# The last V load of a cached-attention decode kernel, cut into parts whose rows are placed on chosen DMA engines

## The chip, the cores and the metric

The kernel runs on one core of a Trainium2 chip. The metric is the device time of one execution in microseconds (us), as the median of several runs. The kernel before takes 1277.13 us (three runs, 1277.09 to 1277.35).

## The reference

One decode step for a batch of four tokens with 512 features: a pre-normed attention over a long key/value cache, then a pre-normed gated feed-forward block, both with a residual.

```python
B, Sq, D = 4, 1, 512;  H, Sk, Dh = 32, 8192, 128;  F = 1792
q = (layernorm(x) @ wq)                                # per head, 128 wide
p = softmax(einsum("bhqd,bhkd->bhqk", q, k_cache) * Dh ** -0.5)
h = x + einsum("bhqk,bhkd->bhqd", p, v_cache) @ wo
n = layernorm(h)
out = h + (sigmoid(n @ w_gate) * (n @ w_up)) @ w_down
```

All inputs are bf16. The two caches hold 4 x 32 x 8192 x 128 elements each, 537 MB together. The weights add 4 MB (wq), 4 MB (wo) and 5.5 MB (gate, up, down).

## The kernel before

The work on the cache is cut into 32 groups g of four heads of one batch item. For each group one K of 8 MB and one V of 8 MB are loaded, each with one DMA instruction from SyncE's queue (SP): 128 partitions, one row of 32768 elements (64 KB) on each. Partition p holds 256 positions of head p // 32 of the group. SBUF holds three such slots (the tensor `KV`, three times `SLOT` = 32768 elements per partition), which K and V loads use in turn. Loads are issued in the order K(0), K(1), V(0), K(2), V(1), K(3) and so on. Each waits for the event that frees its slot: K(g+1) for the end of group g-2's output (`t_ox`, a VectorE instruction), V(g) for group g's softmax maximum (`t_a5`, VectorE), which comes after the last use of K(g).

Of a group, VectorE transposes K in eight pieces (L332), TensorE (PE) makes the scores (L342, 64 matmuls) and, one group later, the product with V (L385, 64 matmuls), and ScalarE and VectorE do the softmax between them. Groups 2 to 30 run in a hardware loop on PE and VectorE.

The end of the program is written out by hand. `load_v(31)` (L299), the last V, waits for the output of group 29 and goes into slot 0. Its DMA counts up a semaphore of its own, `vl`. Then follow, on the same queue, `load_weights`: two halves of wo (L312), w_gate and w_up (L316), which wait for the last softmax maximum, and w_down in four loads (L326: 1 MB, 0.5 MB and twice 128 KB), which wait for the PE product of group 30. PE does the product of group 30 (L385), three filler matmuls (`fill`, L434, which keep PE busy and whose results nobody reads), then `pv_last` (L399), the 64 matmuls on the last V. `pv_last` waits for the last V's semaphore and for the softmax weights. Behind it come, one after the other: `extract_last` (L420 to L426, with a matmul at L424 that needs the tile `RS`, which GpSimd makes late in the program, L504 to L510), the first half of the output projection with wo (L457), fillers, the second half, the second layernorm, w_gate (L560), three fillers, w_up (L560), the gating, the transposed hidden vector (L571) and w_down (L591). The result leaves by a DMA from ScalarE's queue (L603).

GpSimd (POOL) has little to do: it builds identities and masks at the start, makes the masked queries of each group (L282), copies each group's output (L286), and makes `RS` at the end. It issues no DMA.

`_Prog.dma` (L79 on) issues a DMA behind its waits and lets it add 16 to its semaphore; several DMAs on one semaphore add up, and a wait for the last of them waits for all.

Of the kernel before, what the change touches and what calls it, by code (L numbers as in the profile page):

```python
# [5 lines left out]
BF16 = mybir.dt.bfloat16  # L6
FP32 = mybir.dt.float32
# [4 lines left out]
class _Prog:  # L12
# [28 lines left out]
    def emit(self, eng, fn, waits=(), incs=1, key=None, take=(), keep=True):  # L41

        todo = self._waits(eng, waits)
        assert not (todo and self.looped), (eng, todo)
        key = key or eng
        tok = self.token(key, incs) if incs else None

        def run(e):
            for k, v in todo:
                e.wait_ge(self.sems[k], v)  # L50
            for k, v in take:
                e.wait_ge(self.sems[k], v).then_inc(self.sems[k], -v)  # L52
            made = fn(e)
            made = made if isinstance(made, list) else [made]
            if incs:
                assert len(made) == incs
                for m in made:
                    m.then_inc(self.sems[key], 1)

        if keep:  # L60
            self.ops[eng].append(run)
        return tok
# [26 lines left out]
def bass_sequential_preLN__mha_block_cached__glu_gated_glu__decode_kernel(  # L89
# [20 lines left out]
    SLOT = 4 * S * DH // 128  # L110
    SCALE = float(DH) ** -0.5
    EPS = 1e-5
    LW = 144
    PW = 8 * 128 + 32

    prog = _Prog()
    emit = prog.emit

    with ExitStack() as es:
        def SB(name, shape, dt, **kw):  # L120
            return es.enter_context(nc.sbuf_tensor(name, shape, dt, **kw))

        def raw(t):
            return t.tensor if hasattr(t, "tensor") else t

        KV = SB("KV", [128, 3, SLOT], BF16, align_bytes=256)
        Lq = SB("Lq", [128, 4, LW], BF16)
        PT = SB("PT", [128, 3, PW], BF16)
        E_sb = SB("E_sb", [128, 512], BF16)
# [19 lines left out]
        OTs = SB("OTs", [128, 3, 4], BF16)  # L149
        hhT = ET[:, 0:NFT * B]  # L150
        hh = E_sb[:, :]
        dummy = SB("dumm", [128, 2], FP32)

        KVROW = 3 * SLOT

        def kv(slot, off, inner, p0=0, np_=128):
            return bass.AP(raw(KV), p0 * KVROW + slot * SLOT + off, [[KVROW, np_], *inner])
# [10 lines left out]
        FY = (bank[1], FA)  # L168

        keys = ["sp", "act", "dve", "pool", "pe", "x", "out", "cs", "wq", "wo0", "wo1", "wg", "wu", "wd0", "wd1", "wd2", "wd3",  # L170
                "sl0", "sl1", "sl2", "vl", "v0", "v1", "v2", "tp", "pt", "ex", "dv", "sc", "pv", "lq"]
        for k in keys:
            prog.sems[k] = es.enter_context(nc.semaphore("s_" + k))

# [2 lines left out]
        dram_v = lambda g: A_v_cache[g % B, 4 * (g // B):4 * (g // B) + 4, :, :].rearrange(  # L177
            "h (p r) d -> (h p) (r d)", p=32)
# [95 lines left out]
        t_v, t_et, t_pv, t_ox = {}, {}, {}, {}  # L274
# [19 lines left out]
        def load_v(g):  # L294
            last = g == NG - 1
            vslot[g] = slot = 0 if last else (2 * g + 2) % 3
            w = [t_ox[g - 2]] if last else [t_a5[g]] if g else [t_qp]
            if last:
                t_v[g] = [prog.dma("sp", "vl", lambda e: e.dma_start(kv(slot, 0, [[1, SLOT]]), dram_v(g)), w)] * 4  # L299
            else:  # L300
                t_v[g] = [prog.dma("sp", f"v{slot}", lambda e: e.dma_start(kv(slot, 0, [[1, SLOT]]), dram_v(g)), w)] * 4

# [44 lines left out]
        def softmax(g, keep):  # L347
# [14 lines left out]
            for a in range(4):  # L362
                if g < NG - 1:
                    dst = bass.AP(raw(PT), 32 * a * 3 * PW + u3 * PW + 32 * a, [[3 * PW, 32], [128, 8], [16, 2], [1, 16]])
                    src = bass.AP(raw(ET), 32 * a * 512, [[512, 32], [64, 8], [32, 2], [1, 16]])
                else:
                    dst = bass.AP(raw(PT), 32 * a * 3 * PW + u3 * PW + 4 * a, [[3 * PW, 32], [64, 16], [16, 4], [1, 4]])
                    src = bass.AP(raw(ET), 32 * a * 512, [[512, 32], [32, 16], [4, 4], [1, 4]])
# [22 lines left out]
        def pv_last(g):  # L391
            u3, slot = g % 3, vslot[g]
            for j in range(4):
                def f(e, j=j):
                    ins = None
                    for rl in range(NS):
                        off, t = 64 * rl + 16 * j, rl % 4
                        rhs = kv(slot, (4 * j * 16 + rl) * 128, [[2048, 4], [1, 128]])
                        ins = e.matmul(V_b[32 * t:32 * (t + 1), :], PT[:, u3, off:off + 32], rhs,  # L399
                                       start=(j == 0 and rl < 4), stop=(j == 3 and rl >= NS - 4),  # L400
                                       tile_position=(0, 32 * t), skip_group_check=True)
                    return ins
                t_pv[g] = emit("pe", f, [t_v[g][j]], take=[("pt", 4)] if j == 0 else [])

        def extract(g, keep):
            src = bass.AP(raw(PS), 512 * 2, [[4096, 128], [128, 4], [1, 4], [4, 32]])
# [56 lines left out]
        load_k(0)  # L463
        load_k(1)
        load_v(0)
        TURNS = (NG - 2) // 3
        assert 2 + 3 * TURNS == NG
        for g in range(NG):
# [13 lines left out]
            if g > 1:  # L482
                keep_o(g - 2)
                if g + 1 < NG:
                    load_k(g + 1)
                else:
                    load_v(g)
# [3 lines left out]
            if 0 < g < NG - 1:  # L491
                load_v(g)
# [12 lines left out]
        for a in range(4):  # L505
# [5 lines left out]
                SEL[32 * a:32 * a + B, :], identf[32 * a:32 * a + B, 32 * a:32 * a + B]), [t_rs])  # L511
        fill(3, S_b[0], [t_et[NG - 1]])
        pv_last(NG - 1)
        emit("pe", gather(range(3)), [t_oc[27], t_ox[NG - 2]])
        fill(1, S_b[0])
# [83 lines left out]
        def o_half(u):  # L599
# [3 lines left out]
        key, v = prog.dma("act", "out", lambda e: e.dma_start(  # L603
            out.rearrange("b s d -> (b s) d"), kv(0, 0, [[1, D]], 0, B)), [t_o])
# [33 lines left out]
```

## Time and profile before

| what | value |
|---|---|
| median of the runs | 1277.13 us (1277.09 to 1277.35) |
| profiled execution, first to last instruction (span) | 1275.6 us |
| the median over that span (what lies around the instructions) | 1.5 us |
| read from HBM | 550.77 MB, 432 GB/s over the span |
| PE busy | 1001.2 us (78%) |
| VectorE (DVE) busy | 701.8 us (55%) |
| ScalarE (ACT) busy | 85.2 us (7%) |
| GpSimd (POOL) busy | 22.6 us (2%) |
| granted TensorE clock | 0.918 |

The page gives no time of its own for the profiled execution but its span, so a time of a run is compared here with the span and 1.5 us. In the rows of a timeline the first number is the start from the span's beginning and the second the duration, both in us. "SPq" and "ACTq" are the instructions that issue DMAs on those queues. A bracket at a row's end tells how long the engine stood idle before it and what ended that. In the view of DMA issues the last number of a row is the time from the issue to the landing of the whole load. In the view of windows, "DMA share" is the busy share of the core's 16 DMA engines in a stretch; it does not name the engines.

### The profile page before, as it was taken

How to read it: one execution, taken by the hardware profiler on the slowest of the kernel's cores; microseconds unless marked ns; L12 is line 12 of the kernel's file. 1: busy time of each engine (PE TensorE's matmuls, PEld its weight loads, DVE VectorE, ACT ScalarE, POOL GpSimd, SP SyncE). 2: the span in 40 equal slices, each digit the busy share in tenths (PEclk: the TensorE clock that was granted, in tenths of full speed). 3: DMA queues.
4: the chain of work that ended last, by engine and by line, in shares of the span. 5: the costliest groups of instructions: out<-in, count | busy, mean ns of one | idle time of the engine just before them, and what ended most of it. 6: DMA issues, size and time to landing. Idle time of an engine off the chain costs nothing. (4 is left out here: it accounts for less than half of the span.)

```text
span 1275.6 us, 10932 instructions
## 1 busy us (share of the span) xinstructions
PE 1001.2 (78%) x4450; PEld 409.7 (32%) x4450; DVE 701.8 (55%) x737; ACT 85.2 (7%) x202; POOL 22.6 (2%) x88
## 2 busy tenths in 40 slices
PE   1598777779777788777798777797777897777888
PEld 1233323333233333223333233333233332333334
DVE  0865665446655446654456654456554466544562
ACT  0000000000000000000000000000000000000010
POOL 1000000000000000000000000000000000000000
PEclk9899888899888898888998888998888998888989
DMA  9999999999999999999999999999999999999998
GB/s 420 434 425 434 427 444 432 430 438 427 442 434 430 438 427 444 432 432 436 427 444 432 432 436 434 438 432 434 434 434 438 432 436 432 436 436 430 440 430 371
DMA packets 10669, 550.95 MB, mean 432 GB/s; under 512 B 1176, under 2 KB 1440, under 8 KB 1824
## 3 DMA queue, kind: packets, MB, share of 16 engines
q1 hardware_dynamic: 10640, 550.77, 99.8%
q8 instruction: 8, 0.13, 0.0%
q14 instruction: 5, 0.04, 0.0%
q10 hardware_dynamic: 16, 0.01, 0.0%
HBM read 550.77 MB, written 0.00 MB: 432 GB/s over the span
## 5 line engine op out<-in xcount | busy, mean ns | idle before, releaser
L332 DVE STREAM_TRANSPOSE KV<-KV 128x2048 uint32<-128x2048 uint32 x256 | 568.6, 2279 | 379.1 <-DVEq L52 379.1
L342 PE MATMUL PS<-KV,Lq 128*128 128x512 bf16 x2048 | 543.6, 417 | 258.2 <-PEq L52 257.5
L385 PE MATMUL PS<-KV,PT 128*128 128x512 bf16 x1984 | 433.2, 379 | 0.0
L342 PEld LDWEIGHTS PS<-KV,Lq 128*128 128x128 bf16 x2048 | 199.8, 104 | 601.4 <-issue 442.7
L385 PEld LDWEIGHTS PS<-KV,PT 128*128 128x128 bf16 x1984 | 193.8, 98 | 234.5
L358 ACT ACTIVATE E_sb<-PS,TS 128x512 bf16<-128x512 f32 x32 | 22.0, 688 | 1124.6 <-DVE TS L357 1124.6
L352 DVE TENSOR_REDUCE TS<-PS 128x1 f32<-128x512 f32 x32 | 22.1, 692 | 70.4 <-DVEq L52 70.4
L369 ACT ACTIVATE PT<-ET 32x256 bf16<-32x256 bf16 x128 | 52.9, 413 | 30.8 <-DVE ET L361 28.5
L361 DVE STREAM_TRANSPOSE ET<-E_sb 128x512 bf16<-128x512 bf16 x32 | 22.8, 711 | 30.7 <-DVEq L52 30.7
L412 DVE STREAM_TRANSPOSE OX<-PS 128x512 f32<-128x512 f32 x31 | 20.9, 675 | 8.6 <-DVEq L52 8.6
L282 POOL TENSOR_TENSOR Lq<-q_all,mask 128x16 bf16<-128x16 bf16 x32 | 8.4, 263 | 575.0 <-DVE TS L357 563.4
L286 POOL COPY OT<-OTs 128x4 bf16<-128x4 bf16 x30 | 5.8, 192 | 622.3 <-DVE OTs L415 622.3
L434 PE MATMUL PS<-identf 128*128 128x512 f32 (+3 forms) x30 | 13.3, 551 | 0.0
L253 PE MATMUL PS<-xnT,KV 128*128 128x4 bf16 x128 | 3.6, 166 | 9.4 <-DMA KV<-in_A_wq_dram 9.4
L353 DVE STREAM_TRANSPOSE TS<-TS 128x32 f32<-128x32 f32 x32 | 6.8, 211 | 5.1 <-DVEq L52 0.6
L357 DVE STREAM_TRANSPOSE TS<-TS 128x32 f32<-128x32 f32 x32 | 6.8, 211 | 4.7
L374 DVE STREAM_TRANSPOSE TS<-TS 128x32 f32<-128x32 f32 x32 | 6.8, 211 | 4.7
L415 DVE TENSOR_SCALAR OTs<-Or,small 128x4 bf16<-128x4 f32 x30 | 6.9, 229 | 4.5 <-DVEq L52 1.4
L373 DVE COPY TS<-small 128x32 f32<-128x32 f32 x32 | 5.8, 182 | 6.2 <-DVEq L52 3.0
L355 DVE TENSOR_SCALAR TS<-small 128x32 f32<-128x32 f32 x32 | 5.8, 181 | 4.8 <-DVEq L52 0.2
L414 DVE TENSOR_REDUCE Or<-OX 128x4 f32<-128x16 f32 x31 | 5.6, 179 | 4.5
L354 DVE TENSOR_REDUCE small<-TS 128x1 f32<-128x16 f32 x32 | 5.4, 170 | 4.7
(87 smaller groups left out, 78.1 us busy)
## 6 DMA issues: line engine op xcount, KB each, us to landing
KV<-in_A_wq_dram SPq DMA_DIRECT2D x1, 4096.0 KB, 12.4
KV<-in_A_wo_dram SPq DMA_DIRECT2D x2, 2048.0 KB, 22.1
KV<-in_B_w_gate_dram SPq DMA_DIRECT2D x1, 1792.0 KB, 28.2
KV<-in_B_w_up_dram SPq DMA_DIRECT2D x1, 1792.0 KB, 32.0
KV<-in_B_w_down_dram SPq DMA_DIRECT2D x1, 1024.0 KB, 24.2
KV<-in_A_k_cache_dram SPq DMA_DIRECT2D x32, 32.4
KV<-in_A_v_cache_dram SPq DMA_DIRECT2D x32, 34.3
KV<-in_B_w_down_dram SPq DMA_DIRECT2D x1, 512.0 KB, 25.0
```

Source lines behind the costliest of these rows:

```text
L282: emit("pool", lambda e: e.tensor_tensor(dst, src, msk, ALU.mult), [t_q, t_mk, t_lq0, t_a5.get(g - 1), t_oc.get(g - 3)], key="lq")
L332: emit("dve", lambda e: e.transpose(v, v), key="tp", take=take, keep=keep)
L342: ins = e.matmul(S_b[0], Lq[:, hp, 15 - s:15 - s + 128], rhs, start=(s == 0 and hp == 0), stop=(s == NS - 1 and hp == 3))
L352: dv(lambda e: e.tensor_reduce(TS[:, 0, 0:1], S_b[0], AX.X, ALU.max), [t_ts0] if g == 0 else [], [("sc", 1)])
L353: dv(lambda e: e.transpose(TS[:, 1, :], TS[:, 0, :]))
L358: emit("act", lambda e: e.activation(E_sb[:, :], S_b[0], ACT.Exp, bias=TS[:, 3, 0:1], scale=SCALE, accum_out=TS[:, 4, 0:1]), [t_a5[g]], ke ...
L361: t_et[g] = dv(lambda e: e.transpose(ET[:, :], E_sb[:, :]), take=[("ex", 1)], key="dve")
L369: emit("act", lambda e, dst=dst, src=src: e.activation(dst, src, ACT.Copy), [t_et[g], t_pt0 if g < NG - 1 else t_ptl], key="pt")
L385: ins = e.matmul(O_b, PT[:, u3, off:off + 128], rhs, start=(j == 0 and rl == 0), stop=(j == 3 and rl == NS - 1))
L412: emit("dve", lambda e: e.transpose(OX[:, :, :].rearrange("p (r i) x -> p r i x", r=4), src), w, key="dv", take=take, keep=keep)
L415: t_ox[g] = emit("dve", lambda e: e.tensor_scalar(dst, Or[:, :], small[:, 2 + g % 3:3 + g % 3], None, op0=ALU.mult), take=[("dv", 1)], kee ...
L434: ins = e.matmul(bk[:, 0:cols], identf[:, :], bass.AP(raw(identf), 0, [[128, 128], [0, cols // 128], [1, 128]]), start=True, stop=True, sk ...
```

## The change

Only the last V (group 31) is loaded in another way. Its rows are cut at 26624 elements: the first 52 KB of all 128 rows stay one load, and the last 12 KB (`REL` = 6144 elements) of each row go in seven sets of loads.

- From SP, ahead of the large load: rows 7, 15, 23 and 31 in one load, rows 39 and 47 in one, rows 55 and 63 in one.
- From SP, the large load of 128 rows of 52 KB, and behind it the 12 KB ends of the 64 even rows, of the 32 rows 1, 5, 9, ... and of the 16 rows 3, 11, 19, ....
- From GpSimd's queue, twice the sequence: a load of 8 x 4 bytes of x into spare columns of the tile `dummy` (`skip`), the ends of three rows, a load of 4 x 4 bytes of x, the end of one row. The rows are 71, 79, 87 and 95 the first time and 103, 111, 119 and 127 the second. These eight loads count up a new semaphore, `vp`.

So the 16 rows p = 7, 15, 23, ..., 127 have their last 12 KB in small loads. The change's description names DMA engines 0, 1, 8, 9, 10 and 15 as those that they go to. `pv_last` now waits for both semaphores, `vl` and `vp`. The wait of the loads for their slot is the same for SP and GpSimd (the output of group 29). `dummy` grows from two to six columns.

```diff
+    REL = 6 * 1024
...
-        dummy = SB("dumm", [128, 2], FP32)
+        dummy = SB("dumm", [128, 6], FP32)
...
             if last:
-                t_v[g] = [prog.dma("sp", "vl", lambda e: e.dma_start(kv(slot, 0, [[1, SLOT]]), dram_v(g)), w)] * 4
+                src = dram_v(g)
+
+                def part(eng, key, p0, st, n, lo, hi):
+                    dst = bass.AP(raw(KV), p0 * KVROW + slot * SLOT + lo, [[st * KVROW, n], [1, hi - lo]])
+                    return prog.dma(eng, key, lambda e: e.dma_start(
+                        dst, src[p0:p0 + st * (n - 1) + 1:st, lo:hi]), w)
+
+                def skip(n, c):
+                    xs = A_x.rearrange("b s (x d) -> (b s x) d", d=128)
+                    prog.dma("pool", "vp", lambda e: e.dma_start(
+                        dummy[0:n, 2 + c:3 + c].bitcast(BF16), xs[0:n, 0:2]), w)
+                for i in range(2):
+                    skip(8, 2 * i)
+                    part("pool", "vp", 71 + 32 * i, 8, 3, SLOT - REL, SLOT)
+                    skip(4, 2 * i + 1)
+                    t_vp = part("pool", "vp", 95 + 32 * i, 8, 1, SLOT - REL, SLOT)
+                for p0, n in ((7, 4), (39, 2), (55, 2)):
+                    part("sp", "vl", p0, 8, n, SLOT - REL, SLOT)
+                part("sp", "vl", 0, 1, 128, 0, SLOT - REL)
+                for p0, st in ((0, 2), (1, 4), (3, 8)):
+                    t_vl = part("sp", "vl", p0, st, 128 // st, SLOT - REL, SLOT)
+                t_v[g] = [t_vl, t_vp]
...
-                t_pv[g] = emit("pe", f, [t_v[g][j]], take=[("pt", 4)] if j == 0 else [])
+                t_pv[g] = emit("pe", f, t_v[g], take=[("pt", 4)] if j == 0 else [])
```

On SP's queue, at the end of the program, this stood before (the last V is the row with L299):

```order
L299 DMA KV<-in_A_v_cache_dram 128x32768 [waits s_dve]
L312 DMA KV<-in_A_wo_dram 128x8192 [waits s_dve]
L312 DMA KV<-in_A_wo_dram 128x8192
L316 DMA KV<-in_B_w_gate_dram 128x7168
L316 DMA KV<-in_B_w_up_dram 128x7168
```

and this stands there now (partitions x elements; L304 is `part`):

```order
L304 DMA KV<-in_A_v_cache_dram 4x6144 [waits s_dve]
L304 DMA KV<-in_A_v_cache_dram 2x6144 x2
L304 DMA KV<-in_A_v_cache_dram 128x26624
L304 DMA KV<-in_A_v_cache_dram 64x6144
L304 DMA KV<-in_A_v_cache_dram 32x6144
L304 DMA KV<-in_A_v_cache_dram 16x6144
L334 DMA KV<-in_A_wo_dram 128x8192 [waits s_dve]
L334 DMA KV<-in_A_wo_dram 128x8192
```

One issue has become seven, in front of the weights; the weights and their waits are as before.

On GpSimd, between the copy of group 29's output (L286 before, L287 now) and the memset that begins `RS` (L504 before, L526 now), this stood before:

```order
L471 MEMSET PT 128x1056
L286 COPY OT<-OTs 128x4 [waits s_dve]
L504 MEMSET KV 128x644 [waits s_pe]
L507 COPY KV<-identf 32x128 [waits s_pool]
L510 COPY KV<-identf 4x4 [waits s_pool]
```

and this stands there now:

```order
L287 COPY OT<-OTs 128x4 [waits s_dve]
L309 DMA dumm<-in_A_x_dram 8x2
L304 DMA KV<-in_A_v_cache_dram 3x6144
L309 DMA dumm<-in_A_x_dram 4x2
L304 DMA KV<-in_A_v_cache_dram 1x16x384
L309 DMA dumm<-in_A_x_dram 8x2
L304 DMA KV<-in_A_v_cache_dram 3x6144
L309 DMA dumm<-in_A_x_dram 4x2
L304 DMA KV<-in_A_v_cache_dram 1x16x384
L526 MEMSET KV 128x644 [waits s_pe]
```

Eight DMA issues have come in between; a load of a single row is written by the build as 16 pieces of 384 elements. On PE nothing moves; the first matmul of `pv_last` waits for one semaphore more (`s_vp`).

More of the change, by code (lines that the diff above doesn't have):

```diff
@@ L170, in bass_sequential_preLN__mha_block_cached__glu_gated_glu__decode_kernel @@
         keys = ["sp", "act", "dve", "pool", "pe", "x", "out", "cs", "wq", "wo0", "wo1", "wg", "wu", "wd0", "wd1", "wd2", "wd3",
-                "sl0", "sl1", "sl2", "vl", "v0", "v1", "v2", "tp", "pt", "ex", "dv", "sc", "pv", "lq"]
+                "sl0", "sl1", "sl2", "vl", "vp", "v0", "v1", "v2", "tp", "pt", "ex", "dv", "sc", "pv", "lq"]
         for k in keys:
```

## The prediction

> **What bounds the kernel now.** I read the page first, its DMA rows above all.
>
> ```profile
> DMA  9999999999999999999999999999999999999998
> ...
> q1 hardware_dynamic: 10640, 550.77, 99.8%
> q8 instruction: 8, 0.13, 0.0%
> ...
> HBM read 550.77 MB, written 0.00 MB: 432 GB/s over the span
> ```
>
> SP's queue (q1) keeps the 16 DMA engines busy for 99.8% of the span; PE is busy for 78%. The kernel lasts as long as its 550.77 MB take. One engine moves 432 / 16 = 27.0 GB/s. So the change, which moves no byte less, can only gain where engines stand idle. That is at the end, in the view of windows (us of the window, DMA share and GB/s last; GpSimd's busy time stands between):
>
> ```profile
> 1271.20:1271.60 0.40, 0.00 (x0) 1.00 1.03 402
> 1271.60:1272.00 0.40, 0.00 (x0) 1.00 0.67 266
> 1272.00:1272.40 0.40, 0.00 (x0) 1.00 0.61 225
> 1272.40:1272.80 0.40, 0.00 (x0) 1.00 0.57 197
> 1272.80:1273.20 0.40, 0.00 (x0) 1.00 0.34 108
> 1273.20:1273.60 0.40, 0.00 (x0) 1.00 0.00 0
> ```
>
> The last transfers end engine by engine. The share is full until 1271.6, then about 0.67, 0.61 and 0.57, that is 10.7, 9.8 and 9.1 engines of 16; none works after 1273.2. So about five engines are through by 1271.8, seven by 1272.6, and the other nine finish in the last 0.4 to 0.6 us. The idle share of the four stretches is 0.33 + 0.39 + 0.43 + 0.66 = 1.81, by 0.4 us: a mean engine waits 0.72 us for the last one. Perfect levelling would end the transfers 0.72 us earlier and not more.
>
> Next the path from the transfers to the end: the timeline of SP's issues and of PE (PEld loads weights), and in the view of DMA issues the time to landing of the last V and of w_up.
>
> ```profile
> 1218.39 0.33 SPq L299 DMA_DIRECT2D KV<-in_A_v_cache_dram  x1
> ...
> 1237.14 0.43 SPq L316 DMA_DIRECT2D KV<-in_B_w_up_dram  x1
> ...
> 1250.94 3.64 PE L399 MATMUL PS<-KV,PT 128*32 128x512 bf16 x64 [0.97 <-issue]
> ...
> 1266.35 2.84 PE L434 MATMUL PS<-identf 128*128 128x512 f32 x6
> ...
> 1269.15 0.53 PEld L560 LDWEIGHTS PS<-KV,hnT 128*4 128x4 bf16 x16 [0.78 <-DMA KV<-in_B_w_up_dram]
> ```
>
> ```profile
> KV<-in_A_v_cache_dram SPq DMA_DIRECT2D x1, 32.5
> ...
> KV<-in_B_w_up_dram SPq DMA_DIRECT2D x1, 1792.0 KB, 32.0
> ```
>
> The last V lands at 1218.39 + 32.5 = 1250.9, and PE begins on it at 1250.94 after 0.97 us of idleness: here a transfer ends last. From there to the end PE's own chain and the landings keep step. w_up lands at 1237.14 + 32.0 = 1269.1, and the fillers before it end at 1266.35 + 2.84 = 1269.19, so each hides the other. An earlier landing of the weights alone would therefore bring nothing, and an earlier V alone nothing either: both must move. They do move together, since an engine that is ahead in the last V is ahead in everything queued behind it.
>
> **The change, part by part.** *Row ends taken from the engines.* A row end is 6144 x 2 = 12,288 bytes, at 27.0 GB/s 0.455 us. Before, one load of 128 rows of 64 KB gives each engine eight rows. Now each gets the first 52 KB of its eight rows and, from the three loads of 64, 32 and 16 rows, 4 + 2 + 1 = 7 ends: one end less, -0.455 us on every engine. The 16 ends come back by the small loads. The large loads run on 16 engines with equal shares; if a small load of n rows runs on n engines, the SP loads of 4, 2 and 2 rows give two engines three ends each and two more engines one each, and GpSimd's give four engines two ends each. In sum: two engines +0.91 us, four +0.455, two 0, eight -0.455.
>
> The profile names no engine, so that the six receivers are the early ones is the change's statement and not my reading; the counts agree, though. Eight engines are relieved, and eight or nine are late; six receive, and five to seven are early. Early engines finish at about 1271.6, and a receiver of two net ends then finishes at 1272.5, still before the relieved late ones at 1273.2 - 0.455 = 1272.75. The relieved engines stay last, so the term is -0.455 us.
>
> *More loads on a ring.* A late engine works through four loads where it had one. The nearest rows are the small loads of w_down at the end.
>
> ```profile
> 1247.43 1.84 SPq L326 DMA_DIRECT2D KV<-in_B_w_down_dram  x4
> ```
>
> ```profile
> KV<-in_B_w_down_dram SPq DMA_DIRECT2D x1, 512.0 KB, 25.0
> KV<-in_B_w_down_dram SPq DMA_DIRECT2D x2, 128.0 KB, 24.7
> ```
>
> Four issues in 1.84 us are 0.46 each, so the 512 KB load goes out at 1247.89 and lands at 1272.89; the two of 128 KB go out at 1248.35 and 1248.81 and land on average at 1248.58 + 24.7 = 1273.28. The distance of 0.39 us holds one and a half loads of 128 KB, which at 432 GB/s take 1.5 x 0.303 = 0.455. A load boundary thus costs 0 to 0.05 us within the rounding of these rows. Three more: 0 to 0.15; I take 0.05, nearer to nothing, as the sum above came out below the data's own time. The 24 skip pieces of 4 bytes count as nothing.
>
> *One wait more on PE.* Before, PE begins 0.05 us after the last V's landing with two waits. A third, already fulfilled, is 0 to 0.05; I take 0.03. Behind it in PE's order stands all of the tail, so it would count in full.
>
> *SP's six further issues.* Seven issues of 0.33 to 0.46 us from 1218.39 end by 1221.6. The next thing on SP waits for VectorE until 1235.8, and the V before is still in transfer, as these rows show (issue, landing, and PE's use of it):
>
> ```profile
> 1197.21 0.33 SPq L301 DMA_DIRECT2D KV<-in_A_v_cache_dram  x1
> ...
> 1233.43 13.97 PE L385 MATMUL PS<-KV,PT 128*128 128x512 bf16 x64
> ...
> 1235.82 0.80 SPq L312 DMA_DIRECT2D KV<-in_A_wo_dram  x2
> ```
>
> ```profile
> KV<-in_A_v_cache_dram SPq DMA_DIRECT2D x1, 34.3
> ```
>
> It lands at 1197.21 + 34.3 = 1231.5, so no engine runs dry behind the issues: nothing. If GpSimd's row ends slip in ahead of that V on their engines, it is late by at most 0.91 us on engines that are ahead, and PE wants it at 1233.43, 1.9 us later: nothing.
>
> *Eight issues on GpSimd.* The trace of before has no DMA from GpSimd. These rows tell the room:
>
> ```profile
> 1218.43 0.19 POOL L286 COPY OT<-OTs 128x4 bf16<-128x4 bf16 x1 [20.03 <-DVE OTs L415]
> ...
> 1247.46 0.63 POOL L504 MEMSET KV<- 128x644 f32 x1 [28.84 <-PE PS L385]
> ...
> 1250.24 0.18 POOL L510 COPY KV<-identf 4x4 f32<-4x4 f32 x1
> ...
> 1255.69 0.40 PE L424 MATMUL PS<-stx,KV 128*128 128x16 f32 x2
> ```
>
> ```profile
> L197 POOL MEMSET PT<- 128x3168 bf16 x1 | 2.7, 2748 | 0.0
> ```
>
> GpSimd idles from 1218.62 to 1247.46. Behind the eight issues queue the memset and copies of `RS`, which end at 1250.42 and are wanted at 1255.69, so they may slip 5.3 us. The row ends must have landed by 1250.5, when PE would begin. That is 31.9 us for eight issues, 4.0 us each. Bounds: 0.33 us (an issue on SP) and 2.75 us (GpSimd's longest instruction here), 2.6 to 22 us in all: hidden at both ends. [...]
>
> Sum: -0.455 + 0.05 + 0.03 = -0.375 us. The span goes from 1275.6 to 1275.2, and the time, with the 1.5 us around the span, from 1277.13 to **1276.8 us**. The bounds of the unknown terms make it 1276.7 to 1276.9. A measurement of this kernel tells about 0.2%, 2.6 us, from no change; the forecast is inside that, -0.03%.
>
> **Rivals.** *The ends land on other engines than those ahead: no change.* The two loads of one row stand in the program as 16 pieces of 384 elements. [...] The late engines end between 1272.6 and 1273.2, so the gain lies between 0 and the 0.375 of the sum: 1276.8 to 1277.2, and 1277.1 if the last is hit. [...] No row shows engines. Chance 0.26.
>
> *Late engines receive: slower.* Which engines are late has a cause, and if it is a chance one, the order of the profiled execution isn't that of others. The page has eight instruction loads of 0.13 / 8 = 16 KB: each holds one engine 0.6 us, nearly the mean gap. If they, or GpSimd's place in its round, fall otherwise, a late engine gets two ends and ends 0.455 us later (1277.6 with the overheads), or three ends and ends 0.91 us later (1278.1). It decides where a receiver is less than 0.455 or 0.91 us ahead. Against it: the fixed program, and runs that agree within 0.26 us. Chance 0.14.
>
> *GpSimd's loads come late: slower by more than 0.2%.* Over 4.0 us per issue `pv_last` waits for `vp`, and each further 0.5 us on an issue puts 4 us on the end: 4.5 us each give about 1281. For it: no run here shows such a load, and its first one may cost more, which also goes for anything the queue needs at the program's start. Against it: 29 us of idle GpSimd. Chance 0.07.
>
> *Better than the sum,* up to the 0.72 us of perfect levelling (1276.4), or anything unseen: 0.03.
>
> **How the numbers follow.** Forecast 0.50, no change 0.26, late engines 0.14, GpSimd late 0.07, the rest 0.03. The likeliest gives 1276.8. The range of 1276.4 to 1278.1 goes from perfect levelling to a late engine with two net ends more and leaves out the GpSimd case. Faster by over 0.2% would need 2.6 us where at most 0.72 is to be had: 0.01. Slower by over 0.2%: the GpSimd case and a little, 0.08. Within: 0.91.
>
> **What would show it.** In the windows of the profile after, the transfers should end about 0.4 us earlier and more steeply: over 0.8 of the engines busy until half a microsecond before the last. `pv_last` should start at about 1250.55, with the memset of `RS` still at 1247.5. If the last windows fall in the same long steps, the ends went to the wrong engines; if they have a longer tail of one or two engines, late ones received; if `RS` starts late or PE waits for GpSimd's loads, the fourth case holds. The prediction is wrong if the time leaves the range, or if it falls while the steps stay.

## The result, and the profile after

The kernel after takes 1284.25 us (median of five runs, 1283.52 to 1285.25), the kernel before in the same comparison 1277.14 (five runs, 1277.09 to 1277.35). The ratio is 1.0057, with a 95% interval of 1.0045 to 1.0069: 7.1 us slower, where 1276.8 and a range up to 1278.1 had been forecast. The profiled execution has a span of 1282.9 us and took 1284.25. One of the ten executions of the third experiment below took 1399.39 us at a granted clock of 0.66, and nothing is read from it.

The page of the kernel after, DMA queues (packets, MB, share of 16 engines) and rate:

```profile
q1 hardware_dynamic: 10816, 550.67, 99.4%
...
HBM read 550.77 MB, written 0.00 MB: 429 GB/s over the span
```

The bytes are the same, and the engines are as busy as before. So the loss is no idleness: the engines are busy for longer on the same bytes. Where, the windows tell (GpSimd's busy time, granted clock, DMA share, GB/s). First the kernel before, then the kernel after, from just before the landing of the V of group 30 (1231.5 before) to just behind the use of the last V:

```profile
1228.00:1236.00 8.00, 0.00 (x0) 1.00 1.02 442
1236.00:1244.00 8.00, 0.00 (x0) 1.00 0.97 420
1244.00:1248.00 4.00, 0.54 (x1) 1.00 1.10 475
1248.00:1252.00 4.00, 1.95 (x9) 1.00 0.71 303
1252.00:1256.00 4.00, 0.00 (x0) 1.00 1.00 430
1256.00:1260.00 4.00, 0.00 (x0) 1.00 1.00 429
```

```profile
1228.00:1236.00 8.00, 0.00 (x0) 1.00 1.00 338
1236.00:1244.00 8.00, 0.00 (x0) 1.00 1.01 424
1244.00:1248.00 4.00, 0.52 (x1) 1.00 0.91 390
1248.00:1252.00 4.00, 1.96 (x9) 1.00 0.92 315
1252.00:1256.00 4.00, 0.00 (x0) 0.68 1.01 351
1256.00:1260.00 4.00, 0.00 (x0) 0.50 1.00 426
```

A packet counts in the window where it starts, so a single window of before swings (475, then 303, where packets of 64 KB give way to smaller ones); sums over several windows can be compared. There are two dips. From 1228 to 1236 the rate is 338 instead of 442 at a share of 1.00: (442 - 338) x 8 / 432 = 1.9 us lost. From 1244 to 1260 the four rates sum to 1482 instead of 1637: 155 x 4 / 432 = 1.4 us. From 1236 to 1244 nothing is lost. The first dip is where the small loads run, the second where the 12 KB ends of the large loads run. Together 3.3 us of a mean engine.

The packets' own records in the trace say the same. A few of the kernel after, in the first dip and around it (start, us, bytes):

```
1226.34 2.42 65536
1228.60 3.19 65536
1230.75 0.85 12288
1231.24 3.00 53248
1237.50 1.97 53248
```

Undisturbed, 64 KB take 2.42 us, 52 KB 1.97 and 12 KB 0.46. In the dip SP's rows of 12 KB take 0.56 to 0.86, and the packets of 52 and 64 KB that start beside them 1.1 to 1.5 times their time. It isn't only the small loads that are slow.

The timeline of the kernel after, SP's, GpSimd's and PE's rows, and two issues with their time to landing:

```profile
1218.40 4.32 SPq L304 DMA_DIRECT2D KV<-in_A_v_cache_dram  x7
...
1222.34 0.51 POOL L304 DMA_DIRECT2D KV<-in_A_v_cache_dram  x1
...
1247.25 2.74 PE L456 MATMUL PS<-identf 128*128 128x512 f32 x6
1247.45 5.46 SPq L348 DMA_DIRECT2D KV<-in_B_w_down_dram  x4
1247.48 0.63 POOL L526 MEMSET KV<- 128x644 f32 x1 [24.62 <-PE PS L407]
...
1256.67 5.40 PE L421 MATMUL PS<-KV,PT 128*32 128x512 bf16 x64 [6.68 <-PEq L52]
...
1276.61 1.03 PE L582 MATMUL PS<-KV,hnT 128*4 128x512 bf16 x16
```

```profile
KV<-in_B_w_up_dram SPq DMA_DIRECT2D x1, 1792.0 KB, 37.3
```

```profile
KV<-in_A_v_cache_dram POOLq DMA_DIRECT2D x1, 12.0 KB, 28.2
```

`pv_last` starts at 1256.67 instead of 1250.94: 5.73 us later, after 6.68 us of idleness. Its 64 matmuls then take 5.40 us instead of 3.64, another 1.76. The two make 7.5 us, and the span grew by 7.3. Of the 5.73, 3.3 are those of a mean engine. In the packets' records the last row of V ends at 1255.67 instead of 1250.51, 5.16 us later, so some 1.9 us more are the lag of the last engine behind the mean; and PE begins 1.00 us behind that end instead of 0.43, which is the remaining 0.6. GpSimd's last load lands at 1222.34 + 28.2 = 1250.5, so the late landing is SP's. w_up lands at 1237.16 (its issue) + 37.3 = 1274.5 and is used at 1276.61 without a wait: from `pv_last` on PE's own chain sets the end.

Why the matmuls take longer, the windows of PE (busy time, clock, share, GB/s) show: the granted clock was 0.50.

```profile
1252.40:1256.60 4.20, 0.00 (x0) 0.63 0.95 355
1256.70:1260.10 3.40, 3.40 (x36) 0.50 0.99 424
1260.10:1262.00 1.90, 1.90 (x48) 0.95 1.03 441
```

And the end of the transfers, which answers to the first windows of the prediction:

```profile
1274.40:1274.80 0.40, 0.00 (x0) 1.00 0.94 376
1274.80:1275.20 0.40, 0.00 (x0) 1.00 0.66 266
...
1276.80:1277.20 0.40, 0.00 (x0) 1.00 0.09 33
...
1278.00:1278.40 0.40, 0.00 (x0) 1.00 0.07 23
1278.40:1278.80 0.40, 0.00 (x0) 1.00 0.02 8
```

A share of 0.06 is one engine of 16. The transfers end some 5.3 us later than before and less evenly: one engine alone works for the last 1.5 us or so.

### The profile page after: what moved, and what is told of

Its sections match the earlier page's. It is cut to its first block, busy times and chain, and to the rows that moved or that the text cites. A ratio compares the mean times of both kernels' runs of the same rounds, so it can differ in the third digit from the quotient of the medians.

```text
span 1282.9 us, 10947 instructions
## 1 busy us (share of the span) xinstructions
PE 1001.5 (78%) x4450; PEld 409.7 (32%) x4450; DVE 701.8 (55%) x737; ACT 85.2 (7%) x202; POOL 26.8 (2%) x96
## 3 DMA queue, kind: packets, MB, share of 16 engines
q1 hardware_dynamic: 10816, 550.67, 99.4%
## 5 line engine op out<-in xcount | busy, mean ns | idle before, releaser
L287 POOL COPY OT<-OTs 128x4 bf16<-128x4 bf16 x30 | 5.8, 192 | 622.0 <-DVE OTs L437 622.0
L421 PE MATMUL PS<-KV,PT 128*32 128x512 bf16 x64 | 5.4, 512 | 6.7 <-PEq L52 6.7
## 6 DMA issues: line engine op xcount, KB each, us to landing
KV<-in_B_w_up_dram SPq DMA_DIRECT2D x1, 1792.0 KB, 37.3
```

## The experiments

All were timed in three rounds beside the kernel before, whose medians were 1277.08 to 1277.15. The diffs show what stands in place of the loads of the last V in the kernel after. The first four take the change apart.

**Only the cut.**

```
part("sp", "vl", 0, 1, 128, 0, SLOT - REL)
t_v[g] = [part("sp", "vl", 0, 1, 128, SLOT - REL, SLOT)]
```

> The last V as two loads of all 128 rows from SP: the first 52 KB of each row, then the last 12 KB. No small loads, no rows left out by strides. Theory P (the small loads of two to four rows run on engines other than those that carry these rows in a load of 128, and while they are in transfer all engines slow down): nothing of that here, 1277.1 to 1277.3 us. Theory S (loads of every second, fourth or eighth row are slow in themselves): nothing of that either, 1277.1 to 1277.3. Theory G (loads from GpSimd's queue hold up the others): 1277.1 to 1277.3. If the cut at 52 KB itself costs, 1278 or more, and all three are wrong.

Measured: 1277.17 us, ratio 1.0001 (0.9991 to 1.001). To cut the load at 52 KB costs nothing.

**Only the sets of many rows,** all 128 ends by SP (64, 32, 16 and 16 rows), no small loads.

```
part("sp", "vl", 0, 1, 128, 0, SLOT - REL)
for p0, st in ((0, 2), (1, 4), (3, 8), (7, 8)):
    t_vl = part("sp", "vl", p0, st, 128 // st, SLOT - REL, SLOT)
t_v[g] = [t_vl]
```

> As the changed kernel, but the 16 rows 7, 15, ..., 127 go in one more SP load of 16 rows (step 8) behind the others, so that every load uses all 16 engines with equal shares; no small loads, nothing from GpSimd. Theory P: 1277.1 to 1277.4, the transfer rate stays near 432 GB/s to the end of the last V. Theory S: the second stretch of lost rate (about 300 GB/s for four us where the changed kernel changes over to the weights) is still there, 1279 to 1282. Theory G: 1277.1 to 1277.4.

Measured: 1280.74 us, ratio 1.0027 (1.0016 to 1.0039), with windows and the start of `pv_last`:

```profile
1228.00:1236.00 8.00, 0.00 (x0) 1.00 1.01 437
...
1244.00:1248.00 4.00, 0.24 (x1) 1.00 0.80 340
1248.00:1252.00 4.00, 2.24 (x9) 1.00 1.06 287
1252.00:1256.00 4.00, 0.00 (x0) 0.68 0.98 403
```

```profile
1253.23 5.32 PE L414 MATMUL PS<-KV,PT 128*32 128x512 bf16 x64 [2.96 <-issue]
```

The first dip is gone, the second is there: 1208 - (340 + 287 + 403) = 178 against before's three windows, by 4 / 432 = 1.6 us of a mean engine. Counted from its issue (1218.68 here, 1218.39 before), the last V is used 2.0 us later, and here too the clock had fallen (5.32 us instead of 3.64, 1.68 more). Together that is about the 3.66 us by which the run is slower. The packets' records show where it begins (start, us, bytes):

```
1248.08 0.46 12288
1249.42 0.78 12288
1250.05 1.07 16384
1253.99 0.61 16384
```

81 of the 128 ends go through at 0.46 us each, and from 1248.5 to 1252 the packets take 1.5 to 1.7 times their time on average, those of wo (16 KB, 0.61 us) as well; from 1252.8 on they are undisturbed again.

**Only the small loads.** The other 112 ends are not loaded, so 1.38 MB (3.2 us of the transfers) are missing.

```
for i in range(2):
    skip(8, 2 * i)
    part("pool", "vp", 71 + 32 * i, 8, 3, SLOT - REL, SLOT)
    skip(4, 2 * i + 1)
    t_vp = part("pool", "vp", 95 + 32 * i, 8, 1, SLOT - REL, SLOT)
for p0, n in ((7, 4), (39, 2), (55, 2)):
    part("sp", "vl", p0, 8, n, SLOT - REL, SLOT)
t_vl = part("sp", "vl", 0, 1, 128, 0, SLOT - REL)
t_v[g] = [t_vl, t_vp]
```

> As the changed kernel, but without the three loads of 64, 32 and 16 rows: the last 12 KB of these 112 rows are not loaded (1.38 MB less, which alone takes 3.2 us off), so the result of group 31 is not the reference's. The small loads of SP and GpSimd stay. Theory P: the first stretch of lost rate stays, about 2 us of mean engine time and an uneven end: 1276 to 1279. Theory S: 1273.9 to 1274.5. Theory G: like P, 1276 to 1279.

Measured: 1278.20 us, ratio 1.0008 (0.9998 to 1.0018), no gain from 3.2 us of transfers less.

```profile
1228.00:1236.00 8.00, 0.00 (x0) 1.00 0.99 337
```

```profile
1251.83 3.64 PE L419 MATMUL PS<-KV,PT 128*32 128x512 bf16 x64 [1.70 <-PEq L52]
```

The first dip, whole. In the kernel before PE uses the last V 32.55 us after its issue; without a loss it would be about 32.55 - 3.2 = 29.4 here. It was 1251.83 - 1218.55 = 33.3, so the 16 small rows delay it by about 3.9 us: 1.9 are the dip, the rest is the last engine's lag behind the mean. With the 2.0 of the second experiment this is 5.9, near the 5.73 of the whole change (which has one load of 16 rows where that experiment has two): both parts cost.

**No GpSimd.** As the kernel after, with its eight rows left unloaded (0.1 MB).

```
for p0, n in ((7, 4), (39, 2), (55, 2)):
    part("sp", "vl", p0, 8, n, SLOT - REL, SLOT)
part("sp", "vl", 0, 1, 128, 0, SLOT - REL)
for p0, st in ((0, 2), (1, 4), (3, 8)):
    t_vl = part("sp", "vl", p0, st, 128 // st, SLOT - REL, SLOT)
t_v[g] = [t_vl]
```

> As the changed kernel, but without GpSimd's eight loads: the last 12 KB of the rows 71, 79, ..., 127 are not loaded (0.1 MB less, 0.2 us), so the result of group 31 is not the reference's. SP's three small loads and the strided loads stay. Theory P: about half of the first stretch goes, 1279 to 1282. Theory S: 1279 to 1282, mostly from the second stretch. Theory G: 1277 or less.

Measured: 1281.87 us, ratio 1.0042 (1.0028 to 1.0057).

```profile
1228.00:1236.00 8.00, 0.00 (x0) 1.00 0.96 369
```

```profile
1254.67 4.93 PE L416 MATMUL PS<-KV,PT 128*32 128x512 bf16 x64 [4.43 <-issue]
```

Theory G, that it is GpSimd's loads, falls: without them 4.8 of the 7.1 us remain (of the 2.3 that go, the bytes left out make 0.2), and the first dip is still (442 - 369) x 8 / 432 = 1.4 us of its 1.9. Neither P nor S holds alone, since both halves of the change lose time. What they share had to be found. The next four ask whether it is the number of loads, the source or the destination, that is, which partitions are written together.

**No load of 16 rows:** the same rows 3, 7, 11, ... by one load of 32 rows.

```
part("sp", "vl", 0, 1, 128, 0, SLOT - REL)
for p0, st in ((0, 2), (1, 4), (3, 4)):
    t_vl = part("sp", "vl", p0, st, 128 // st, SLOT - REL, SLOT)
t_v[g] = [t_vl]
```

> As e2_strided_only, but the last 32 rows (3, 7, 11, ...) go in one load of 32 rows (step 4) instead of two of 16 rows (step 8). [...] Theory B (HBM side: 16 engines that read at a pitch of 512 KB in step hit the same memory channels): the pitch is 256 KB at most, two reads apart, so also 1277.1 to 1277.5, or half the loss, 1279. Theory C (every load with fewer than 128 rows is slow, or engines that work on different loads at once disturb each other): 1279 to 1281 as e2.

Measured: 1277.61 us, ratio 1.0003 (0.9994 to 1.0013), just above the range of 1277.1 to 1277.5, and far from theory C's 1279 to 1281.

```profile
1244.00:1248.00 4.00, 0.52 (x1) 1.00 0.79 337
1248.00:1252.00 4.00, 1.96 (x9) 1.00 1.03 437
1252.00:1256.00 4.00, 0.00 (x0) 1.00 1.02 438
```

The three sum to 1212, before's to 1208: nothing is lost, and of the 210 large packets that start between 1246 and 1253 none takes over 1.05 times its undisturbed time. PE uses the last V 32.58 us after its issue (32.55 before). Strided ends and three loads more on the queue are harmless to the transfers, so theory C falls; the two loads of 16 rows with step 8 make the second dip.

**16 rows from near sources:** the same partitions as in the second experiment, but the sources of the two loads are 16 rows that follow one another (so other data).

```
def near(p0, st, n, s0):
    dst = bass.AP(raw(KV), p0 * KVROW + slot * SLOT + SLOT - REL, [[st * KVROW, n], [1, REL]])
    return prog.dma("sp", "vl", lambda e: e.dma_start(dst, src[s0:s0 + n, SLOT - REL:SLOT]), w)
part("sp", "vl", 0, 1, 128, 0, SLOT - REL)
for p0, st in ((0, 2), (1, 4)):
    part("sp", "vl", p0, st, 128 // st, SLOT - REL, SLOT)
near(3, 8, 16, 0)
t_v[g] = [near(7, 8, 16, 16)]
```

> As e2_strided_only, with the same partitions written by the two loads of 16 rows, but their sources are the ends of rows 0 to 15 and 16 to 31, 64 KB apart instead of 512 KB (so the result of group 31 is not the reference's). [...] Theory B: the loss is gone, 1277.1 to 1277.5. Theory C: 1279 to 1281.

Measured: 1280.01 us (1278.41 to 1280.93), ratio 1.0021 (1.0011 to 1.003).

```profile
1248.00:1252.00 4.00, 2.04 (x9) 1.00 1.06 286
```

```profile
1252.86 3.64 PE L418 MATMUL PS<-KV,PT 128*32 128x512 bf16 x64 [2.79 <-issue]
```

The dip stays at 286 GB/s. In this profiled execution (1278.72) PE waited 2.79 us and kept its clock; that the runs lie in two groups, near 1278.6 and near 1280.5, fits a clock that fell in some of them only (so does the second experiment, with one run of seven at 1278.87 and the others from 1280.32 to 1281.59), but those runs have no trace.

**Far sources:** a tail load of 128 rows whose sources lie 512 KB apart (other data), at contiguous partitions.

```
part("sp", "vl", 0, 1, 128, 0, SLOT - REL)
far = A_v_cache.rearrange("b h (p r) d -> (b h p) (r d)", p=32)
dst = bass.AP(raw(KV), slot * SLOT + SLOT - REL, [[KVROW, 128], [1, REL]])
t_v[g] = [prog.dma("sp", "vl", lambda e: e.dma_start(dst, far[0:1017:8, SLOT - REL:SLOT]), w)]
```

> As e1_cut_only, with the second load of 128 row ends taken from rows that lie 512 KB apart in the V cache instead of 64 KB (so the result of group 31 is not the reference's); the partitions are written as in e1. [...] Theory B: lost rate over the whole load of 1.5 MB, which at the 255 to 300 GB/s seen in e2 takes 1.5 to 2.5 us more: 1278.5 to 1280. Theory C: 1277.1 to 1277.5.

Measured: 1277.18 us, ratio 1.0 (0.9991 to 1.001). Both runs on the source agree: theory B, which had 1277.1 to 1277.5 for the sixth (1280.01) and 1278.5 to 1280 for this one, falls. What is left is the destination.

**Small loads on other partitions.** As the third experiment (112 ends not loaded), but with the small rows on 3, 7, 11, 15; 35, 39; 2, 6 (SP) and 67, 71, 75, 95; 99, 103, 107, 127 (GpSimd).

```
-    part("pool", "vp", 71 + 32 * i, 8, 3, SLOT - REL, SLOT)
+    part("pool", "vp", 67 + 32 * i, 4, 3, SLOT - REL, SLOT)
-for p0, n in ((7, 4), (39, 2), (55, 2)):
-    part("sp", "vl", p0, 8, n, SLOT - REL, SLOT)
+for p0, n in ((3, 4), (35, 2), (2, 2)):
+    part("sp", "vl", p0, 4, n, SLOT - REL, SLOT)
```

> [...] Theory B or C, or GpSimd's loads slow by themselves: as e3, 1277.5 to 1279.

Measured: 1276.39 us, ratio 0.9994 (0.9985 to 1.0004), against 1278.20 for the same loads on the change's partitions.

```profile
1228.00:1236.00 8.00, 0.00 (x0) 1.00 1.00 411
```

```profile
1247.46 2.74 PE L454 MATMUL PS<-identf 128*128 128x512 f32 x6
1250.28 3.64 PE L419 MATMUL PS<-KV,PT 128*32 128x512 bf16 x64
```

The same number of loads, rows and bytes, from the same queues: with other partitions alone (their source rows change with them, which the sixth and seventh experiments clear) the first dip shrinks from 1.9 to (442 - 411) x 8 / 432 = 0.6 us. The last row of V ends 31.2 us after the issue, 1.6 us earlier than in the third experiment, but 2.2 later than even shares without a loss would have it: the dip's 0.6 leaves 1.6 for the last engine's lag. The 1274 to 1275.5 us that I had expected if the destination decides were missed for another reason: `pv_last` follows the fillers without idleness. PE's chain is the floor here, and an earlier last V can't bring more than the 0.97 us that PE waited in the kernel before.

**Contiguous sets of rows,** a second test of the destination: the sets of the second experiment as blocks (rows 0 to 63, 64 to 95, 96 to 111, 112 to 127).

```
part("sp", "vl", 0, 1, 128, 0, SLOT - REL)
for p0, n in ((0, 64), (64, 32), (96, 16), (112, 16)):
    t_vl = part("sp", "vl", p0, 1, n, SLOT - REL, SLOT)
t_v[g] = [t_vl]
```

> As e1_cut_only, with the last 12 KB loaded in four loads of neighbouring rows: 0 to 63, 64 to 95, 96 to 111 and 112 to 127. The sources lie as near as they can (64 KB apart), the engines have equal shares. [...] Theory B (HBM side, pitch): 1277.1 to 1277.6. Theory C (any load of fewer rows is slow): about as e2, 1279 to 1281.

Measured: 1285.76 us, ratio 1.0067 (1.0051 to 1.0084).

```profile
1244.00:1248.00 4.00, 0.56 (x1) 1.00 0.89 236
1248.00:1252.00 4.00, 1.92 (x9) 1.00 1.04 208
1252.00:1256.00 4.00, 0.00 (x0) 0.91 1.02 167
```

With the same counts of rows and the same bytes the last V is now used 7.1 us late instead of 2.0. The rate falls to about half of 432 GB/s (208 to 236) in the blocks of 64 and 32 rows and below that (167) in those of 16. For the blocks of 16 the windows are mixed: from 1252 to 1256, at 167 GB/s, packets of wo run beside the last ends, and both take 2.6 to 2.7 times their undisturbed time on average; so a rate of these blocks alone is not shown here.

**More fillers.** The kernel after with ten fillers instead of three before `pv_last`.

```
-        fill(3, S_b[0], [t_et[NG - 1]])
+        fill(10, S_b[0], [t_et[NG - 1]])
```

> The changed kernel with ten filler matmuls instead of three ahead of the product with the last V, so that PE works until about 1256.4 us, just short of the 1256.67 at which it began on the last V. Theory K (of the 7.1 us lost, 1.8 are not the transfer's: PE stands idle for 6.7 us, its granted clock falls to 0.5, and the 64 matmuls take 5.40 us instead of 3.64): 1282.3 to 1282.9 us, and the matmuls take 3.64 again. Rival (the matmuls are slow for another reason, or the landings are what ends last behind them): 1283.8 to 1284.8, as the changed kernel.

Measured: 1282.8 us (1282.55 to 1282.93), ratio 1.0044 (1.0027 to 1.0061).

```profile
1247.22 8.75 PE L456 MATMUL PS<-identf 128*128 128x512 f32 x20
1256.91 3.64 PE L421 MATMUL PS<-KV,PT 128*32 128x512 bf16 x64 [0.94 <-issue]
```

Theory K holds: with PE kept busy the matmuls take 3.64 us again. That saves 1.45 us of the 7.1, as the V landed 0.24 later here. The rest is the late landing.

**Only the skip loads.** The last V in one load as before, with GpSimd's four loads of a few bytes, for which PE waits.

```
for i in range(2):
    skip(8, 2 * i)
    t_vp = (skip(4, 2 * i + 1), ("vp", prog.count["vp"]))[1]
t_v[g] = [prog.dma("sp", "vl", lambda e: e.dma_start(kv(slot, 0, [[1, SLOT]]), dram_v(g)), w), t_vp]
```

> The kernel before with its single load of the last V, and beside it only GpSimd's four skip loads of 4-byte pieces, for which PE waits too. [...] Rival from the prediction (a queue on GpSimd costs something at the program's start or in its issues): 1278 or more.

Measured: 1277.13 us, ratio 1.0 (0.9991 to 1.001). GpSimd's queue, its issues and PE's third wait cost nothing. Yet its loads of 4 bytes a piece are long on their way:

```profile
dumm<-in_A_x_dram POOLq DMA_DIRECT2D x2, 0.0 KB, 12.1
dumm<-in_A_x_dram POOLq DMA_DIRECT2D x2, 0.0 KB, 15.9
```

## Why the prediction was wrong, point by point

**"Row ends taken from the engines": the step that failed.** It priced a row end at 0.455 us on the engine that carries it, and took the engines as the only thing that is shared. Equal shares of a large load are shown: in the kernel before the 128 packets of 64 KB that start from 1212.0 to 1231.4 us follow one another, end to start, in 16 chains of eight. Which engines the small loads run on was its assumption, after the change's statement; no run shows it. The term was put at -0.455 us; the last V was used 5.73 us later instead. An undisturbed end does take 0.46 us. But at a DMA share of 1.0 the rate still depended on which partitions were written together: from 1248 to 1252 it was 437 GB/s in the fifth experiment and 287 in the second. The sets of 64 and 32 rows with steps 2 and 4 cost nothing (fifth). Rows 3, 11, 19, ... in one load of 16 and 7, 15, 23, ... in another, the same rows as in the fifth's last load of 32, cost 2.0 us at the use of the last V (second). The small loads cost about 3.9 us (third); with the same loads on other partitions two thirds of their dip go (eighth: 1.9 to 0.6 us). That the destination decides is shown. By what means it does is not: no record names the engine of a packet or what engines share on the way into SBUF. Neither loss is a matter of the source (sixth, seventh), of GpSimd's queue alone (fourth, eleventh) or of the number of loads (first, fifth).

The price is larger than a slowing of these two loads alone makes it. At half rate (208 to 236 GB/s were measured in the blocks of 64 and 32 rows) two loads of 16 rows would cost an estimated 2 x 0.455 = 0.9 us more; measured are 1.6 us of a mean engine, since the packets of wo that run beside them take about 1.7 times their time too (1.07 us instead of 0.61). So they hold up packets of other loads; by what means, no run here shows.

**What it did to the view of levelling.** The prediction read the idle share at the end, 0.72 us, rightly as the most that could be had. It misread how many engines are late: in the packets' records of the kernel before, five engines end between 1271.6 and 1271.9 and eleven between 1272.7 and 1273.2, where it counted seven and nine. Of the six receivers that the change names at least one was then a late engine, which by the prediction's own price (0.455 us or more) would have ended at 1273.1 or later, so hardly a gain was left even without the lost rate. The change trades at most 0.72 us against 5.73 us of a later last V. The eighth experiment adds that PE would have given no more than 0.97 back in any case.

**"One wait more" and the chain on PE.** The wait costs nothing that the eleventh experiment shows (1277.13 against 1277.15). But the text has no word on what PE does if it waits for longer: 6.68 us of idleness cost the clock, and 1.76 us more. In the sixth experiment 2.79 us of idleness left the clock whole (3.64 us for the 64 matmuls), while in the second 2.96 already cost most of them their speed (5.32 us). What differs is where the idleness lies. In the clock records of all thirteen traces the clock changes only at points that lie a multiple of 3.41 us apart. Cut at these points (PE's busy time, granted clock, DMA share, GB/s), the second experiment shows

```profile
1250.02:1253.43 3.41, 0.45 (x5) 1.00 0.99 308
1253.43:1256.84 3.41, 3.41 (x36) 0.50 1.02 435
```

and the sixth

```profile
1247.94:1251.36 3.42, 2.13 (x5) 1.00 1.10 297
1251.36:1254.77 3.41, 1.91 (x36) 1.00 0.95 377
```

In the second the idleness fell into one stretch, which was busy for 0.45 us, and the clock was halved in the next, although PE was at work again; in the sixth it fell into two, busy for 2.13 and 1.91 us, and the clock stayed. Over all thirteen traces, of the stretches at full clock, the 399 before a fall had PE busy for at most 43% of the time and the 3504 others for at least 41%: less than about 1.4 us of work (0.41 x 3.41) in one stretch cost the clock in the next.

**"More loads on a ring": right.** 0.05 was taken for three boundaries, and three make the last V late by 0.03 (fifth). The run's time is 0.47 us longer, which the interval does not tell from no change; only 0.1 of it lies in the span, the rest around it (1.9 us instead of 1.5, as in the third and eighth experiments), for which no run shows a cause.

**SP's and GpSimd's issues: hidden, as said.** SP's seven take 4.32 us, 0.62 each instead of 0.33 to 0.46, and end at 1222.7, later than the 1221.6 that was said but long before the next issue at 1235.8. GpSimd's take 0.51 to 0.71 us, inside the bounds of 0.33 and 2.75, and 4.3 us in all; the memset of `RS` starts at 1247.48 (1247.46 before). The landing was no easy success, though: 1250.5 is the very limit that the prediction set, and only the late SP loads hide it.

**The rivals.** None had the mechanism. "GpSimd's loads come late" gave a time over 1280 by a cause that the trace excludes: the last of them landed at 1250.5, and PE waited until 1256.67. "Late engines receive" has its sign in the last windows, one engine alone for some 1.5 us, but its price of at most 0.91 us is far too small. "The ends land on other engines" can be weighed by the packets: each large load adds its rows and 16 more to q1's count (first: 10784 - 10640 = 128 + 16). The kernel after has 10816 - 10640 = 176, which is 120 rows more, 48 for three more large loads, and 8 for small loads of four, two and two rows. So each row of SP's small loads went as one piece, and the eight further packets fit one engine per row. GpSimd's two loads of a single row went as 32 pieces of 768 bytes, as the build had written them; that rival starts from this. Which engine took what is not in these records, so whether the late engines were relieved stays open; at 0.455 us a row it could not have shown beside 5.7.

**What stays open.** Single-row loads (16 pieces of one row) and loads of several rows were not separated in the first dip. A version with all ends loaded that levels the engines without the lost rate was not tried; at most 0.72 us is to be had by it.

## What to carry to other kernels

Where the DMA share is full but GB/s fall, ask which partitions are being written together, not only which queues and engines work. If a load is cut into sets of rows, measure the rate of each set. Here steps 1, 2 and 4 over all 128 partitions kept it (437 to 446 GB/s from 1248 to 1252 in the fifth and seventh experiments); step 8 (287), blocks of 64 and 32 rows (208 to 236) and a few picked rows beside a large load (337 instead of 442 from 1228 to 1236, third experiment) did not. Price a moved row by what it does to all engines. When a wait ahead of PE may grow to over 2 us (an estimate, 3.41 less 1.4), price in that the clock may be halved for the 3.41 us or more that follow, or keep PE busy over it (ninth: 3.64 us instead of 5.40).

## What the runs showed of the hardware that had not been expected

- The last 384 KB of V, in two sets of 16 rows with step 8, slowed the packets in flight, other loads' too, by 1.5 to 1.7 on average (12 KB: 0.46 to 0.78 us; 16 KB of another load: 0.61 to 1.07).
- The granted clock changed only at points a multiple of 3.41 us apart, and fell where PE had been busy for less than about 0.42 of the stretch before (399 falls and 3504 stretches without one, in thirteen traces).
- Sources 512 KB apart cost nothing for a load of 128 rows of 12 KB (1277.18 us, and 1277.17 with 64 KB between them).
- GpSimd's loads of 4 bytes took 12 to 16 us to land beside SP's queue of 64 KB rows, and the last of its rows of 12 KB 28.2 us.
- SP's four issues of w_down took 5.46 us instead of 1.84 in the kernel after, for which no cause was tested; nothing waited for it.
